# Three instead of four VectorE steps to narrow a weight in the first network, and sums of y on GpSimd

## The chip, the cores and the metric

The kernel runs on one core of one Trainium2 chip, in one launch. The metric is the device time of that launch in microseconds; the median of three runs of the kernel before is 980.27 (979.51 to 982.97).

## The reference

Three stages follow one another; the change is about the weights of the second.

```python
# 1: attention, q k v of (2, 8, 576, 64), with a bias from positions
scores = q @ k.T / 8 + relu(x @ w1 + b1) @ w2
x = softmax(scores) @ v                      # as (1152, 512)
# 2: first network: w_in (512, 2048), w_out (2048, 512), a of 4, b of 2
h = x @ w_in
P = a[0] + a[1]*h + a[2]*h**2 + a[3]*h**3
Q = 1 + abs(b[0])*abs(h) + abs(b[1])*h**2
y = (P / (Q + 1e-6)) @ w_out
# 3: four experts, each w1 (512, 1024) and w2 (1024, 512)
out = sum(p[:, e:e+1] * (relu(y @ w1[e]) @ w2[e]) for e in range(4))
```

w_in and w_out reach the kernel as float64 (their values are float32 times a float64 scale), so on the chip each weight is two 32-bit words. The kernel has to narrow each to a float32 and then to split that into a high and a low part of the matmul type, since every product is three matmuls: high by high, high by low, low by high.

## The kernel before

Every engine's instructions stand in the order in which the Python code records them (manual_schedule), and each engine takes its own in that order. TensorE is called PE, VectorE DVE, ScalarE ACT, GpSimd POOL, and SP issues the DMAs.

**Narrowing** (`Piece.narrow`). A piece of a weight is loaded as `words`, low and high word side by side. Four steps of a piece make the float32 in the tile `narrow`, and a fifth, `split` (L434, L435), writes the two parts: ACT copies the high part, POOL subtracts for the low part. For the 14 weights that are narrowed in the first network (pieces of 128 x 1024):

- step 0: ACT takes Abs of the high words, read as floats (L421);
- step 1: DVE takes the maximum with a small constant (L423, the max step), then shifts left by 3 and clears the upper two bits (L424, the mask step);
- step 2: DVE shifts the low words right by 29 and joins them (L426, the low-word step);
- step 3: DVE joins the upper two bits of the high words (L428, the high-word step).

The first two weights are narrowed early, during attention, in six pieces of one row block each (four of 128 x 256, two of 128 x 512). There step 0 is ACT's Square of the high words into a tile `size` (L418) and DVE's mask step out of `words` (L419), steps 1 and 2 are the low-word and the high-word step, and step 3 sets to zero what was too small (L430, with `size`). `EARLY` gives each step of each piece a unit of the attention; `early_convert` calls it, and with step 2 it asks for the load of the next piece, into the same buffer, which waits until the last reader of the words before is done.

**First network.** 24 units (`units`, index i), each one chunk c of 384 tokens and one block f2 of 256 columns of w_in. A unit is 24 matmuls of `hp` (`first`), then ACT and DVE steps on 128 x 768 elements, then 24 matmuls of `yp` two units later (`second`, LAG = 2). Per unit, in the order of the code: ACT L898 and L899 (qd and u out of hp), ACT L837 and POOL L838 for the unit before (its g, high and low part), DVE L903, L904, L905, ACT L906, L907 and L909 (Abs, Ln, Exp, which give 1/Q), then `convert(STEPS[i][0])`, the matmuls `yp` and `gather`, then DVE L919, L920, L921 (g), then `convert(STEPS[i][1])`. L921 is the last reader of hp, of which there are two buffers, so the matmuls of unit i + 2 wait for it. `convert(n)` takes the next n steps of five of the weight that is due; (3, 2) is one whole weight in a unit: three steps ahead of L919, the split and the next weight's step 0 behind L921. That is so in 12 units (2, 3, 4, 6, 7, 9, 10, 11, 14 to 17); units 0 and 1, and 12 and 13, share one weight each; 5 and 8 have none; from 18 on the float32 weights of the experts are split.

**Sums of y** (`gather`). A chunk's yp in PSUM is added up over a run of units, and then goes to `yacc`. In the first run of a chunk ACT copies it there (L861), in the last DVE adds it out of PSUM (L863) and `result` splits the sum for the experts (L875, L876). In the three runs between (they are gathered in units 8, 12 and 14) ACT copies four times into `new` (L868) and DVE adds two pairs (L871, 128 x 768).

**Third stage.** From about 578 us on PE runs without gaps through the experts.

```python
    STEPS = [(3, 2) if i in (2, 3, 4, 6, 7, 9, 10, 11, 14, 15, 16, 17) else (0, 5 * (i > 17)) for i in range(len(units) + LAG)]
    STEPS[:2] = (2, 0), (1, 2)
    STEPS[12:14] = (2, 0), (1, 2)
```

## Time and profile before

| what | value |
|---|---|
| three runs | 979.51, 980.27, 982.97 us |
| profiled execution: its own time, its span | 981.26 us, 979.3 us |
| PE busy | 880.0 us, 90% |
| DVE busy | 563.9 us, 58% |
| ACT busy | 464.3 us, 47% |
| POOL busy | 191.4 us, 20% |
| mean granted PE clock | 0.958 |

The span goes from the first to the last instruction that the profiler recorded; the execution's own time is 1.96 us longer. Busy shares are averages over stages with different limits. A row of the timeline gives start, length, engine, line, operation, tiles written and read, their shapes and how many instructions run together; the bracket behind it gives the idle time of the engine ahead of the row and what ended it. Where the next instruction of an engine starts before the one ahead has ended, the distance of the starts is what counts.

### The profile page before, as it was taken

Reading aid. Unit: us, or ns where it says so; the run is one execution under the profiler, and the core shown is the slowest. Engines: PE = TensorE matmul, PEld = TensorE weight load, DVE = VectorE, ACT = ScalarE, POOL = GpSimd, SP = SyncE. Lnnn points to the kernel's source line nnn. Section 1 sums busy time; section 2 is a strip of 40 time slices with the busy share of each in tenths; the row PEclk is TensorE's granted clock in tenths of the full one; section 3 lists DMA queues with packets and bytes.
Section 4 is the critical chain, followed back from the end, with each engine's and each line's share of the span. In section 5 each row is a group of like instructions: output and inputs, shape, how many; then the busy total and the mean of one; then the engine's idle time right before and its main releaser. Section 6 shows DMA issues by size and latency. Waiting matters only on the chain.

```text
span 979.3 us, 13056 instructions
## 1 busy us (share of the span) xinstructions
PE 880.0 (90%) x5012; PEld 821.5 (84%) x5012; DVE 563.9 (58%) x876; ACT 464.3 (47%) x771; POOL 191.4 (20%) x217
## 2 busy tenths in 40 slices
PE   6866775799999969988979989999999999999998
PEld 6866774699888869877879989998998899889987
DVE  3666775588999788888989974122222331232111
ACT  3735554589888677866767643122211121121000
POOL 3000013475554433424343210000000000000000
PEclk7978897799999979999999999999999999999999
DMA  4255556423231212213130212012201210020000
GB/s 109 61 142 148 182 202 174 113 56 73 63 87 44 87 43 87 86 53 120 48 126 22 65 44 86 1 44 65 65 1 41 67 65 1 24 63 7 27 33 33
DMA packets 72553, 69.92 MB, mean 71 GB/s; under 512 B 42412, under 2 KB 51116, under 8 KB 72492
## 3 DMA queue, kind: packets, MB, share of 16 engines
q1 hardware_dynamic: 72492, 69.09, 23.7%
q8 instruction: 40, 0.66, 0.3%
q14 instruction: 21, 0.17, 0.1%
HBM read 45.48 MB, written 2.36 MB: 49 GB/s over the span
## 4 chain that ended last, share of the span: by engine, by line
PE 53%; DVE 22%; DMA 10%; ACT 9%; SPq 3%; issue 3%; DVEq 0%; ACTq 0%
PE hp L66 23%; PE op L66 20%; PE bps L66 5%; DMA bc<-ev 3%; DMA xt<-in_c_x_dram 3%; DMA ba<-ev 2%; DVE pq L524 2%; DVE narrow L426 2%; DVE u L905 2%; DVE qd L903 2%; DVE pt L565 2%; DVE narrow L428 2%; DVE u L904 2%; PE sc L66 2%; SPq L298 2%
## 5 line engine op out<-in xcount | busy, mean ns | idle before, releaser
L66 PE MATMUL hp<-x,wi 128*128 128x384 f32 x1656 | 295.6, 336 | 24.0 <-DVE u L921 24.0
L66 PEld LDWEIGHTS hp<-x,wi 128*128 128x128 f32 x1656 | 288.5, 189 | 29.2 <-issue 27.3
L66 PE MATMUL op<-w,h_hi 128*128 128x512 f32 (+1 forms) x592 | 178.4, 384 | 0.0
L884 ACT ACTIVATE h_hi<-hp 128x768 fp32r<-128x768 f32 x48 | 39.1, 814 | 246.5 <-PE hp L66 246.5
L885 DVE SCALAR_TENSOR_TENSOR h_lo<-hp,h_hi 128x768 fp32r<-128x768 f32 x48 | 46.0, 958 | 156.3 <-ACT h_hi L884 156.3
L66 PEld LDWEIGHTS op<-w,h_hi 128*128 128x128 f32 x592 | 110.0, 188 | 21.4
L66 PE MATMUL bps<-mask,wb 128*128 128x288 f32 x472 | 84.8, 344 | 36.2 <-DVE mask L254 21.8
L66 PE MATMUL op<-w,h_lo 128*128 128x512 f32 (+1 forms) x296 | 113.7, 384 | 0.0
L66 PEld LDWEIGHTS bps<-mask,wb 128*128 128x128 f32 x472 | 78.9, 229 | 40.6 <-ACT ev L281 14.4
L66 PE MATMUL yp<-g_hi,w 128*128 128x384 f32 x384 | 101.7, 335 | 1.7 <-ACT y L868 1.6
L956 DVE SCALAR_TENSOR_TENSOR acc<-op,pr_sb,acc 128x512 f32<-128x512 f32 (+1 forms) x28 | 20.5, 732 | 112.8 <-PE op L66 112.8
L66 PE MATMUL sc<-ks,qs 128*128 128x288 f32 x320 | 63.5, 327 | 10.4 <-DVE nm L524 7.2
L66 PEld LDWEIGHTS yp<-g_hi,w 128*128 128x128 f32 x384 | 69.7, 188 | 2.7 <-ACT y L868 2.2
L66 PEld LDWEIGHTS op<-w,h_lo 128*128 128x128 f32 x296 | 55.6, 188 | 11.0
L254 DVE TENSOR_SCALAR mask<-lw,thr 128x576 fp32r<-128x576 f32 x118 | 55.9, 524 | 14.5 <-PE bps L66 13.7
L66 PE MATMUL yp<-g_lo,w 128*128 128x384 f32 x192 | 64.2, 334 | 0.0
L66 PEld LDWEIGHTS sc<-ks,qs 128*128 128x128 f32 x320 | 47.5, 199 | 17.5 <-DVE nm L524 10.5
L838 POOL TENSOR_TENSOR g_lo<-u,g_hi 128x768 fp32r<-128x768 f32 x24 | 44.7, 1861 | 89.3 <-ACT g_hi L837 59.7
L281 ACT ACTIVATE ev<-bps 128x576 f32<-128x576 f32 x59 | 38.4, 650 | 48.6 <-PE bps L66 35.2
L524 DVE CUSTOM_DVE_ANT_0 pq<-sc,ba 128x576 f32<-128x576 f32 x72 | 53.8, 749 | 8.1 <-PE sc L66 6.3
L534 ACT ACTIVATE pq<-pq,nm 128x576 f32<-128x576 f32 x72 | 55.4, 769 | 4.2 <-DVE nm L524 3.8
L565 DVE TENSOR_TENSOR pt<-tp,pt 128x512 fp32r<-128x512 f32 x72 | 49.2, 684 | 9.0 <-ACT pt L564 8.4
(134 smaller groups left out, 1279.6 us busy)
## 6 DMA issues: line engine op xcount, KB each, us to landing
stage<-in_moe_w_dram SPq DMA_DIRECT2D x32, 512.0 KB
ba<-ev SPq DMA_DIRECT2D x32, 288.0 KB
bc<-ev SPq DMA_DIRECT2D x32, 288.0 KB
words<-in_moe_w_in_dram SPq DMA_DIRECT2D x7, 1024.0 KB
words<-in_moe_w_out_dram SPq DMA_DIRECT2D x7, 1024.0 KB
raw_q<-in_q_dram SPq DMA_DIRECT2D x32, 128.0 KB
raw_k<-in_k_dram SPq DMA_DIRECT2D x16, 128.0 KB
raw_v<-in_v_dram SPq DMA_DIRECT2D x16, 128.0 KB
```

The costliest lines, as they stand in the source:

```text
L66: pe.matmul(o, lhsT=l, rhs=r, start=start, stop=stop)
L254: dve.tensor_scalar(mk, win, at, None, ALU.is_gt)
L281: act.activation(e_out, sc[:, :, :288], AF.Copy)
L298: sp.dma_start(dst[:, h], ev[r:r + 29:4])
L426: dve.scalar_tensor_tensor(out=u, in0=lo, scalar=29, in1=u, op0=ALU.logical_shift_right, op1=ALU.bitwise_or)
L524: dve.tensor_tensor_reduce(out=self.row(u).rearrange("p (a j) -> p a j", a=2), in0=sc[:, :, :288], in1=bs.rearrange("p (a j) -> p a j", a= ...
L534: act.activation(self.row(u), self.row(u), AF.Exp, bias=least.pop((self.n, u)), scale=-1.0, accum_out=self.sm[b][:, u - 4 * b:u - 4 * b + 1])
L565: dve.tensor_tensor(lo, tp, f32(hi), ALU.subtract)
L838: pool.tensor_tensor(lo, u, f32(hi), ALU.subtract)
L884: act.activation(hi, h, AF.Relu)
L885: dve.scalar_tensor_tensor(out=lo, in0=h, scalar=0.0, in1=f32(hi), op0=ALU.max, op1=ALU.subtract)
L956: dve.scalar_tensor_tensor(out=acc[:, j, cols], in0=op, scalar=pr_sb[:, j, e:e + 1], in1=acc[:, j, cols], op0=ALU.mult, op1=ALU.add)
```

## The change

Step by step:

- Abs on ACT gets a scale of 2**-111, so that what was too small falls to zero by itself. The max step goes, and the mask step clears one bit instead of two. This form now serves the early pieces too: Square, `size` and the step with L430 go, and their mask step moves from step 0 to step 1, the low-word step from 1 to 2, the high-word step from 2 to 3. A tile `gap` takes the room of `size`.
- Weights come out 2**8 too large. The constants of P and Q absorb that: one DVE instruction on them becomes four, one ACT instruction two. What leaves yp is scaled by 2**-8, in the instructions that copied or added it anyway.
- The adds of L871 go from DVE to POOL.
- `STEPS[0]` goes from (2, 0) to (0, 2): in unit 0 the mask and the low-word step come behind L921 instead of ahead of L919.

```diff
--- before.py
+++ after.py
@@ -22,7 +22,7 @@
 E, FE = 4, 1024
 EXP_AND_LN = [s.name for s in SETS].index("natural_log_exp_and_others")
 
-LEAST, ZERO = (float(np.array(x, np.uint32).view(np.float32)) for x in (0x38100000, 0x38000000))
+SHIFT, WUP = 2.0 ** -111, 2.0 ** 8
 P = 128
 NPAIR = H // 2
 LW_W = 2 * S - 1
@@ -405,29 +405,25 @@
 
         def narrow(self, step):
 
+
+
+
+
+
             if not self.w.w64:
                 return
-            tile_of = lambda name: pools["w"].tile(self.shape, F32, tag=name, name=name, bufs=pools["words"] if name == "narrow" else 1)
             if step == 0:
-                self.raw = tile_of("narrow")
+                self.raw = pools["w"].tile(self.shape, F32, tag="narrow", name="narrow", bufs=pools["words"])
             lo, hi = self.words[:, :, :, 0], self.words[:, :, :, 1]
             st, u = self.raw, self.raw.bitcast(U32)
-
-            if step == 0 and self.early:
-                self.size = tile_of("size")
-                act.activation(self.size, hi.bitcast(F32), AF.Square)
-                dve.tensor_scalar(u, hi, 3, 0x3FFFFFFF, ALU.logical_shift_left, ALU.bitwise_and)
-            elif step == 0:
-                act.activation(st, hi.bitcast(F32), AF.Abs)
-            if step == 1 and not self.early:
-                dve.tensor_scalar(st, st, ZERO, None, ALU.max)
-                dve.tensor_scalar(u, u, 3, 0x3FFFFFFF, ALU.logical_shift_left, ALU.bitwise_and)
-            if step == 2 - self.early:
+            if step == 0:
+                act.activation(st, hi.bitcast(F32), AF.Abs, scale=SHIFT)
+            if step == 1:
+                dve.tensor_scalar(u, u, 3, 0x7FFFFFFF, ALU.logical_shift_left, ALU.bitwise_and)
+            if step == 2:
                 dve.scalar_tensor_tensor(out=u, in0=lo, scalar=29, in1=u, op0=ALU.logical_shift_right, op1=ALU.bitwise_or)
-            if step == 3 - self.early:
-                dve.scalar_tensor_tensor(out=u, in0=hi, scalar=0xC0000000, in1=u, op0=ALU.bitwise_and, op1=ALU.bitwise_or)
-            if step == 3 and self.early:
-                dve.scalar_tensor_tensor(out=st, in0=self.size, scalar=LEAST * LEAST, in1=st, op0=ALU.is_ge, op1=ALU.mult)
+            if step == 3:
+                dve.scalar_tensor_tensor(out=u, in0=hi, scalar=0x80000000, in1=u, op0=ALU.bitwise_and, op1=ALU.bitwise_or)
 
         def split(self):
             t = self.w.t[:, self.rows]
@@ -483,6 +479,7 @@
     qkv0, sp_, pt1, qk1, ap, pools["w"], qkv1, sums = (pool_of(name) for name in ("qkv0", "scores", "pt1", "qk1", "attn", "early", "qkv1", "sums"))
     qkv = (qkv0, qkv0), (qk1, qkv1)
     sums.tile([P, 136], F32, name="gap", bufs=1)
+    pools["w"].tile([P, 512], F32, name="gap", bufs=1)
     pt0 = pool_of("pt0")
     pools["words"] = 1
 
@@ -764,8 +761,11 @@
     sp.dma_start(cb_sb, cb.unsqueeze(0).to_broadcast([P, 2]))
     cst = const.tile([P, 8], F32, name="cst")
     nca, abs_b, one = cst[:, 0:4], cst[:, 4:6], cst[:, 6:7]
-    dve.tensor_scalar(nca, ca_sb, -1.0, None, ALU.mult)
-    act.activation(abs_b, cb_sb, AF.Abs)
+
+    for j in range(4):
+        dve.tensor_scalar(nca[:, j:j + 1], ca_sb[:, j:j + 1], -WUP ** -j, None, ALU.mult)
+    for j in range(2):
+        act.activation(abs_b[:, j:j + 1], cb_sb[:, j:j + 1], AF.Abs, scale=WUP ** -(j + 1))
     dve.memset(one, 1.0 + 1e-6)
 
     def ready(w):
@@ -827,7 +827,7 @@
     g_of, y_of = {}, {}
 
     STEPS = [(3, 2) if i in (2, 3, 4, 6, 7, 9, 10, 11, 14, 15, 16, 17) else (0, 5 * (i > 17)) for i in range(len(units) + LAG)]
-    STEPS[:2] = (2, 0), (1, 2)
+    STEPS[:2] = (0, 2), (1, 2)
     STEPS[12:14] = (2, 0), (1, 2)
 
     def parts(i):
@@ -858,17 +858,17 @@
         for d in range(4):
             ya = yacc[:, d, CHN * c:CHN * c + CHN]
             if i == first_end[c]:
-                act.activation(ya, yp[d][:, :CHN], AF.Copy)
+                act.activation(ya, yp[d][:, :CHN], AF.Copy, scale=1 / WUP)
             elif i == last_end[c]:
-                dve.tensor_tensor(ya, ya, yp[d][:, :CHN], ALU.add)
+                dve.scalar_tensor_tensor(out=ya, in0=yp[d][:, :CHN], scalar=1 / WUP, in1=ya, op0=ALU.mult, op1=ALU.add)
                 later.append(lambda ya=ya, yt=x_t[d][:, c]: result(ya, yt))
             else:
                 if d % 2 == 0:
                     new = tmp("y")
-                act.activation(new[:, d % 2], yp[d][:, :CHN], AF.Copy)
+                act.activation(new[:, d % 2], yp[d][:, :CHN], AF.Copy, scale=1 / WUP)
                 if d % 2:
                     ya = yacc[:, d - 1:d + 1, CHN * c:CHN * c + CHN]
-                    dve.tensor_tensor(ya, ya, new, ALU.add)
+                    pool.tensor_tensor(ya, ya, new, ALU.add)
 
     def result(ya, yt):
 
```

What this moves is shown at three places. First POOL in the first network, from the low part of g of unit 11 to that of unit 14; `wi` is the low part of a weight (L435, now L431), `yacc` and `y` belong to the adds. Before:

```order
L838 TENSOR_TENSOR g_lo<-u,g_hi 128x768 x2
L435 TENSOR_TENSOR wi<-narrow,wi 128x4x256
L838 TENSOR_TENSOR g_lo<-u,g_hi 128x768
L435 TENSOR_TENSOR wi<-narrow,wi 128x4x256
L838 TENSOR_TENSOR g_lo<-u,g_hi 128x768
```

And now:

```order
L838 TENSOR_TENSOR g_lo<-u,g_hi 128x768
L871 TENSOR_TENSOR yacc<-yacc,y 128x2x384 x2
L838 TENSOR_TENSOR g_lo<-u,g_hi 128x768
L431 TENSOR_TENSOR wi<-narrow,wi 128x4x256
L838 TENSOR_TENSOR g_lo<-u,g_hi 128x768
L871 TENSOR_TENSOR yacc<-yacc,y 128x2x384 x2
L431 TENSOR_TENSOR wi<-narrow,wi 128x4x256
L838 TENSOR_TENSOR g_lo<-u,g_hi 128x768
```

The two adds of unit 12 now stand between the g_lo of unit 11 and that of unit 12 (those of unit 8 in the same way ahead of its g_lo); the two of unit 14 stand ahead of the low part of a weight and of g_lo.

Second DVE in units 0 and 1, from the first step of unit 0 on. Before:

```order
L903 SCALAR_TENSOR_TENSOR qd<-qd,cst,hp 128x768
L904 TENSOR_TENSOR u<-hp,u 128x768
L905 SCALAR_TENSOR_TENSOR u<-u,cst,hp 128x768
L423 TENSOR_SCALAR narrow<-narrow 128x1024
L424 TENSOR_SCALAR narrow<-narrow 128x1024
L426 SCALAR_TENSOR_TENSOR narrow<-words,narrow 128x1024
L919 SCALAR_TENSOR_TENSOR qd<-qd,hp 128x768
L920 SCALAR_TENSOR_TENSOR hp<-u,cst,hp 128x2x384
L921 SCALAR_TENSOR_TENSOR u<-qd,hp 128x768
L903 SCALAR_TENSOR_TENSOR qd<-qd,cst,hp 128x768
```

And now (the mask step is now L422, the low-word step L424):

```order
L903 SCALAR_TENSOR_TENSOR qd<-qd,cst,hp 128x768
L904 TENSOR_TENSOR u<-hp,u 128x768
L905 SCALAR_TENSOR_TENSOR u<-u,cst,hp 128x768
L919 SCALAR_TENSOR_TENSOR qd<-qd,hp 128x768
L920 SCALAR_TENSOR_TENSOR hp<-u,cst,hp 128x2x384
L921 SCALAR_TENSOR_TENSOR u<-qd,hp 128x768
L422 TENSOR_SCALAR narrow<-narrow 128x1024
L424 SCALAR_TENSOR_TENSOR narrow<-words,narrow 128x1024
L903 SCALAR_TENSOR_TENSOR qd<-qd,cst,hp 128x768
```

L921 of unit 0 has lost the narrowing ahead of it, and L903 of unit 1 now has two steps of it ahead.

Third ACT in the attention, where the fourth early piece is split and the fifth begins; the brackets name the engines whose semaphores an instruction waits for (DMAHW is a load). Before:

```order
L434 ACTIVATE w<-narrow 128x256 [waits DVE_49]
L534 ACTIVATE pq,sm<-pq,nm 128x576 [waits DVE_49,Activation_49]
L564 ACTIVATE pt<-tp 128x4x128 [waits PE_49]
L195 ACTIVATE qs<-tp_q 128x640 [waits PE_49]
L418 ACTIVATE size<-words 128x512 [waits DMAHW1_49]
L534 ACTIVATE pq,sm<-pq,nm 128x576 [waits DVE_49]
```

And now:

```order
L430 ACTIVATE w<-narrow 128x256 [waits DVE_49]
L531 ACTIVATE pq,sm<-pq,nm 128x576 [waits DVE_49,Activation_49]
L561 ACTIVATE pt<-tp 128x4x128 [waits PE_49]
L195 ACTIVATE qs<-tp_q 128x640 [waits PE_49]
L420 ACTIVATE narrow<-words 128x512 [waits DMAHW1_49,Pool_49]
L531 ACTIVATE pq,sm<-pq,nm 128x576 [waits DVE_49]
```

The step writes `narrow` itself, of which there is one in the attention, so it waits for POOL's subtraction of the piece before; until now DVE's L419 did.

## Rows read from the trace of the kernel before

**Rows 1.** Busy time by engine, 380 to 480 us.

```profile
core 0: us, PE busy (x) PEld busy (x) DVE busy (x) ACT busy (x) POOL busy (x), PEclk, DMA share, GB/s
380.00:480.00 100.00, 85.75 (x481) 82.49 (x480) 88.46 (x95) 72.19 (x89) 36.61 (x18) 1.00 0.23 76
```

**Rows 2.** Timeline of DVE, unit 11 and the first step of unit 12.

```profile
452.84 1.01 DVE L903 SCALAR_TENSOR_TENSOR qd<-qd,cst,hp 128x768 f32<-128x768 f32 x1 [1.03 <-ACT u L899]
...
455.69 0.69 DVE L423 TENSOR_SCALAR narrow<-narrow 128x1024 f32<-128x1024 f32 x1
456.41 0.69 DVE L424 TENSOR_SCALAR narrow<-narrow 128x1024 uint32<-128x1024 uint32 x1
...
458.40 1.23 DVE L428 SCALAR_TENSOR_TENSOR narrow<-words,narrow 128x1024 uint32<-128x1024 uint32 x1
...
463.43 1.02 DVE L903 SCALAR_TENSOR_TENSOR qd<-qd,cst,hp 128x768 f32<-128x768 f32 x1 [1.02 <-ACT u L899]
```

**Rows 3.** Timeline of ACT, end of unit 11.

```profile
459.65 1.06 ACT L434 ACTIVATE wi<-narrow 128x1024 fp32r<-128x1024 f32 x1 [2.98 <-DVE narrow L428]
460.62 1.11 ACT L421 ACTIVATE narrow<-words 128x1024 f32<-128x1024 f32 x1
```

**Rows 4.** Timeline of PE, the matmuls hp that start in unit 10.

```profile
451.95 4.42 PE L66 MATMUL hp<-x,wi 128*128 128x384 f32 x24 [2.09 <-DVE u L921]
```

**Rows 5.** The tile narrow over the whole span: durations as min/median/max in ns.

```profile
L423 DVE TENSOR_SCALAR narrow<-narrow x14: 684/686/689, 348.3 to 516.7; 128x1024 f32<-128x1024 f32 x14
...
L419 DVE TENSOR_SCALAR narrow<-words x6: 281/353/855, 244.7 to 320.8; 128x256 uint32<-128x256 uint32 x4, 128x512 uint32<-128x512 uint32 x2
L430 DVE SCALAR_TENSOR_TENSOR narrow<-size,narrow x6: 414/821/1057, 251.3 to 327.7; 128x256 f32<-128x256 f32 x4, 128x512 f32<-128x512 f32 x2
```

**Rows 6.** Timeline of DVE: adds of units 8, 12, 14, and the unit behind each.

```profile
427.06 1.83 DVE L871 TENSOR_TENSOR yacc<-yacc,y 128x768 f32<-128x768 f32 x2 [1.73 <-ACT y L868]
...
431.59 1.01 DVE L903 SCALAR_TENSOR_TENSOR qd<-qd,cst,hp 128x768 f32<-128x768 f32 x1
...
468.87 1.82 DVE L871 TENSOR_TENSOR yacc<-yacc,y 128x768 f32<-128x768 f32 x2
...
473.40 1.01 DVE L903 SCALAR_TENSOR_TENSOR qd<-qd,cst,hp 128x768 f32<-128x768 f32 x1
...
488.04 1.82 DVE L871 TENSOR_TENSOR yacc<-yacc,y 128x768 f32<-128x768 f32 x2
...
492.57 1.01 DVE L903 SCALAR_TENSOR_TENSOR qd<-qd,cst,hp 128x768 f32<-128x768 f32 x1
```

**Rows 7.** Timeline of ACT: u of unit 9, copies of y in unit 14.

```profile
428.44 1.02 ACT L899 ACTIVATE u<-hp,cst 128x768 f32<-128x768 f32 x1
...
485.12 1.62 ACT L868 ACTIVATE y<-yp 128x384 f32<-128x384 f32 x4
```

**Rows 8.** Timeline of DVE: L876 in unit 19, and once more behind unit 23.

```profile
539.82 3.60 DVE L876 TENSOR_TENSOR x<-yacc,x 128x384 fp32r<-128x384 f32 x4
...
588.40 1.96 DVE L876 TENSOR_TENSOR x<-yacc,x 128x384 fp32r<-128x384 f32 x4
```

**Rows 9.** Timeline of POOL, unit 19.

```profile
540.15 1.92 POOL L838 TENSOR_TENSOR g_lo<-u,g_hi 128x768 fp32r<-128x768 f32 x1 [7.14 <-ACT g_hi L837]
```

**Rows 10.** Timeline of PE, the matmuls hp of unit 2.

```profile
353.95 6.75 PE L66 MATMUL hp<-x,w 128*128 128x384 f32 x24 [7.50 <-DVE u L921]
```

**Rows 11.** Timeline of DVE, start of unit 2.

```profile
362.55 1.01 DVE L903 SCALAR_TENSOR_TENSOR qd<-qd,cst,hp 128x768 f32<-128x768 f32 x1 [1.99 <-ACT u L899]
```

**Rows 12.** Timeline of ACT: Square of the third and the fifth early piece.

```profile
271.24 0.43 ACT L418 ACTIVATE size<-words 128x256 f32<-128x256 f32 x1
...
299.49 0.68 ACT L418 ACTIVATE size<-words 128x512 f32<-128x512 f32 x1
```

**Rows 13.** Timeline of POOL: subtraction of the fourth early piece.

```profile
299.52 0.74 POOL L435 TENSOR_TENSOR w<-narrow,w 128x256 fp32r<-128x256 f32 x1
```

**Rows 14.** Timeline of SP: issue of the third early piece's load.

```profile
266.64 0.35 SPq L401 DMA_DIRECT2D words<-in_moe_w_in_dram  x1
```

**Rows 15.** Busy time by engine, behind the second piece's load (issued at 249.57).

```profile
252.00:253.00 1.00, 0.69 (x6) 0.43 (x4) 1.00 (x4) 0.69 (x3) 0.50 (x2) 1.00 0.01 2
```

## The prediction

> **What bounds the kernel now.** I read the chain that ended last first: through attention it changes hands all the time, from about 345 to 578 us it runs through VectorE and ScalarE, and behind that through PE alone, without a gap. So a microsecond gained in the first network arrives at the end whole, and one gained in the third stage could only come from PE, which the change does not touch. Then I read the busy time in the first network: between 380 and 480 us DVE is busy 88%, PE 86%, ACT 72% and POOL 37% [rows 1]. Two engines are close; which one ends last is told by the waits. PE waits 2.09 us for DVE's last step of a unit before it may write hp again [rows 4], in a unit of 10.59 us (452.84 to 463.43, [rows 2]), so it needs some 8.5 us per unit and is not the bound. DVE waits 1.02 us per unit for ACT's u [rows 2], and ACT before that had waited 2.98 us for DVE's high-word step [rows 3]. That is a loop: first step of a unit on DVE, its three steps, the narrowing steps, the high-word step (458.40), ACT's split (459.65), ACT's Abs for the next weight (460.62), ACT's two reads of hp, first step of the next unit (463.43). A narrowing step on DVE lies on it in full; L919 to L921 lie beside it.
>
> **The change, part by part.**
>
> The max step. From its start to that of the mask step are 455.69 to 456.41, 0.72 us [rows 2], on the loop. It runs 14 times with hardly any spread [rows 5]: 12 in the units that narrow a whole weight, one each in units 0 and 12, which are counted below. 12 x 0.72 = **8.64 us**. What is next is the rest of the same loop, 9.87 us per unit, still over PE's 8.5. The mask step keeps its form, and the scale in Abs is an immediate, so I price it at nothing: Abs lies on the loop, and if a scale made it longer, each hundredth of a microsecond would cost 0.14 in all.
>
> The adds in unit 8, where nothing is narrowed. They hold DVE from 427.06 and unit 9 begins at 431.59 [rows 6]. Without them ACT's u is last: it starts at 428.44 and takes 1.02 [rows 7], so unit 9 begins at 429.5, **2.1 us** earlier. PE gets L921 earlier by as much and is then back to back for a unit, which its spare time in the units around covers.
>
> The adds in unit 12. Unit 13 begins at 473.40 without any wait in its row, so DVE was last there. The two adds (1.82 us, overlapping by about 0.08) and the max step leave: 1.74 + 0.72 = **2.46 us**.
>
> The adds in unit 14. Unit 15 too began when DVE came free (492.57, [rows 6]). Without adds and max step, the loop ends last: the high-word step would start at about 488.04 - 1.2 - 0.72 = 486.1, and from its start to the next unit are 458.40 to 463.43, 5.03 us [rows 2], so 491.2. But POOL now adds just then. The second copy of y ends about 486.0 (four of some 0.4 us from 485.12, [rows 7]), so the first add is waiting when the low-word step ends, ahead of the high-word step. What that does is shown by L876, a DVE instruction with two inputs in SBUF like the high-word step: four of them take 1.96 us alone and 3.60 while POOL subtracts g_lo (540.15 for 1.92), which came when the first of them was running [rows 8, 9]. The extra 1.64 us are nearly all of POOL's instruction: POOL went ahead of the second one, which then waited for it. I take the same here: add of 1.86 us from 486.1, high-word step at 487.95, unit 15 at 487.95 + 5.03 = 492.98, 0.41 later than before instead of the 0.72 earlier counted above, a correction of **+1.13 us**. That DVE gets its turn ahead of the second add I take from symmetry; no row shows it.
>
> The Trainium skill says the same against this move in general: in "GPSIMD Engine Reference", section 8, GpSimd shares its SBUF interfaces with VectorE and contends with VectorE instructions that have two SBUF inputs or run in a two-port mode. It names no order and no price. If by that rule the high-word step stood behind both adds, unit 15 would begin 1.9 later still and the sum below would be 11.3 instead of 13.2; the rows are with it as far as L876 goes.
>
> g_lo behind the adds. In unit 8 the adds (two of 1.86 from 427.1) end at 430.8, and g_lo follows until 432.7; the mask step of unit 9 would start at 429.5 + 2.84 = 432.3 (2.85 is 452.84 to 455.69, [rows 2]). If it waits like L876, **+0.3 us**. In unit 12 the adds end near 472 and g_lo is due then. The yp matmuls, which need g_lo, stand behind a whole hp on PE in both places.
>
> Unit 0. The mask and the low-word step (456.41 to 458.40, 1.99 us, [rows 2]) move behind L921. PE's hp of unit 2 waits 7.50 us for that L921 [rows 10], and unit 2 begins at 362.55 after ACT's u [rows 11]. L921 comes some 1.5 us earlier (2.7 of narrowing less the wait for Exp). Unit 1 starts about 0.35 later, and its high-word step with it; from there the loop takes 5.03 as above, so unit 2 begins at about 356.9 + 5.03 = 361.9: **0.6 us** gained, bounds 0 and 1.5.
>
> Attention. DVE loses L430, six of 0.41 to 1.06 us, median 0.82, and has the mask step (0.28 to 0.86, [rows 5]) one step later, in the place of the low-word step, and so on. At most all six count: 4.9 us; but PE, ACT and DVE share the chain here. Against it stand two waits. ACT's Abs now waits for POOL's subtraction of the piece before: the fifth piece's would start at 299.49, POOL is busy from 299.52 for 0.74 [rows 12, 13], so 0.8 us, in ACT ahead of an Exp for which PE waits. And the next piece's load is released by the high-word step, now one step later, with the loads of q and k behind it in SP's queue; these are due a whole pair of heads later. For the third piece, the one with the fewest units between, it goes out not at 266.64 [rows 14] but at about 268.6, 2.6 us before the Abs at 271.24 [rows 12]; the second's load, issued at 249.57, was through by 252.0 (DMA share 0.01 from there, [rows 15]), 2.4 us. It just fits. I take **0.8 us** gained, one L430, between a loss of 0.8 and a gain of 4.9. The longer instructions on the constants stand where ACT and DVE wait for PE: nothing; without that cover some 0.5.
>
> Sum: 8.64 + 2.1 + 2.46 - 1.13 - 0.3 + 0.6 + 0.8 = 13.2 us. The profiled execution's own time, 981.26, becomes 968.1; it lies 1.0 above the median of the runs, so I predict **967.1**.
>
> **The rivals.**
>
> A. More is gained (0.20): the high-word step slips in ahead of POOL in unit 14 (1.8 more), the mask step of unit 9 does not wait (0.3), and three L430 count instead of one (1.7): 963.3. For it: the margin in unit 14 is only 0.1 us. Against: L876 waited.
>
> B. Another engine becomes the bound (0.17): PE's 8.5 per unit against DVE's and ACT's short units 5, 8 and 12, or POOL, which passes the adds' time on to g_lo and the weights. Then the adds (4.6 us with the max step of unit 12) bring nothing, and about 8.5 remain: 971.8. Against: PE's 2.09 us of waiting per unit and POOL's 37%.
>
> C. The change does not do on the loop what I say (0.06): Abs with a scale, or the copies with a scale, take longer and the max step's 0.72 is eaten in good part. 0.5 us more on each Abs would leave 13.2 - 7 = 6; 0.7 leave 3.4: 977.
>
> D. Slower (0.02): in attention, ACT's new wait for POOL. It decides if POOL's queue is late: five pieces have one before them, and each wait would have to reach 3.6 us to turn 13.2 into a loss of 5, about 985. The subtraction of the fourth piece is only 0.77 late for it [rows 12, 13].
>
> **How the numbers follow.** My forecast has 0.55, A 0.20, B 0.17, C 0.06, D 0.02. A measurement of this kernel tells about 0.5%, 4.9 us, from no change. Forecast, A and B are faster by more: 0.92; C within: 0.06; D slower: 0.02. The ends of the unknown costs put together are 13.2 + 2.1 + 4.1 + 0.9 = 20.3 and 13.2 - 1.9 - 1.6 - 0.6 = 9.1 us; all at one end at once is unlikely above, so the range goes from 962 to 972, which takes in A and B.
>
> **What would show it.** The distance from one first step of a unit to the next is about 9.9 in units 2, 3, 10 and 15, with DVE still waiting 1.0 us for ACT's u, and PE's wait for L921 at about 1.4; units 8 and 12 take 7.1 and 7.5 us. In unit 14 the high-word step lasts about 3 us instead of 1.2, and the unit some 11.6; a high-word step of 1.2 there is rival A. Unit 2 begins 0.6 earlier against unit 0. In attention ACT waits for POOL at the fifth piece, and the first network starts 0.8 earlier. I am wrong if the units stay at 10.6, or if PE stops waiting for L921.

## The result, and the profile after

The changed kernel takes 964.89 us (median of four runs, 961.70 to 966.89) beside 979.89 for the kernel before: ratio 0.9861, 95% interval 0.9825 to 0.9897, so 15.0 us less; forecast were 13.2 less and 967.1. In the profiled execution (its own time 963.71, span 961.8) TensorE is still the busiest engine; DVE is busy 13.8 us less and POOL, which has the adds now, 11.0 us more. The page's busy times and its row for the matmuls of hp:

```profile
PE 878.7 (91%) x5012; PEld 821.6 (85%) x5012; DVE 550.1 (57%) x853; ACT 463.6 (48%) x772; POOL 202.4 (21%) x223
...
L66 PE MATMUL hp<-x,wi 128*128 128x384 f32 x1656 | 294.3, 335 | 13.8 <-DVE u L921 13.7
```

The second row is the one that tells: PE's idle time ahead of hp (its last two numbers), nearly all of it put down to DVE's L921, was 24.0 us and is 13.8. The same row of the kernel before:

```profile
L66 PE MATMUL hp<-x,wi 128*128 128x384 f32 x1656 | 295.6, 336 | 24.0 <-DVE u L921 24.0
```

By engine and stretch, a hundred microseconds of the first network, units 2 to 13 (those of [rows 1] were 3 to 13):

```profile
362.00:462.00 100.00, 92.82 (x522) 89.71 (x521) 87.89 (x92) 79.26 (x103) 46.78 (x23) 1.00 0.26 85
```

DVE stays at 88% although each unit asks less of it, since the units are shorter; POOL went from 37 to 47%. One whole-weight unit on DVE, unit 10, which answers to [rows 2]:

```profile
431.50 1.01 DVE L903 SCALAR_TENSOR_TENSOR qd<-qd,cst,hp 128x768 f32<-128x768 f32 x1 [1.11 <-ACT u L899]
...
434.35 0.69 DVE L422 TENSOR_SCALAR narrow<-narrow 128x1024 uint32<-128x1024 uint32 x1
435.07 1.22 DVE L424 SCALAR_TENSOR_TENSOR narrow<-words,narrow 128x1024 uint32<-128x1024 uint32 x1
436.33 1.23 DVE L426 SCALAR_TENSOR_TENSOR narrow<-words,narrow 128x1024 uint32<-128x1024 uint32 x1
...
441.38 1.01 DVE L903 SCALAR_TENSOR_TENSOR qd<-qd,cst,hp 128x768 f32<-128x768 f32 x1 [1.05 <-ACT u L899]
```

From first step to first step 9.88 us, with the same wait of 1.05 for ACT's u at its end: the loop is the same, one step shorter. PE's wait, 2.09 in [rows 4], is now 1.32 ahead of the hp that starts in unit 11, a unit of 9.87 (in unit 10, two behind the short unit 8, it is 0.72):

```profile
450.37 1.82 PE L66 MATMUL hp<-x,wi 128*128 128x384 f32 x9 [1.32 <-DVE u L921]
```

Unit 14 is the place where DVE and POOL meet. Timeline of DVE and then of POOL there:

```profile
466.71 1.02 DVE L903 SCALAR_TENSOR_TENSOR qd<-qd,cst,hp 128x768 f32<-128x768 f32 x1 [1.11 <-ACT u L899]
...
470.28 1.23 DVE L424 SCALAR_TENSOR_TENSOR narrow<-words,narrow 128x1024 uint32<-128x1024 uint32 x1
471.54 2.81 DVE L426 SCALAR_TENSOR_TENSOR narrow<-words,narrow 128x1024 uint32<-128x1024 uint32 x1
...
478.23 1.01 DVE L903 SCALAR_TENSOR_TENSOR qd<-qd,cst,hp 128x768 f32<-128x768 f32 x1 [1.10 <-ACT u L899]
```

```profile
471.42 4.64 POOL L871 TENSOR_TENSOR yacc<-yacc,y 128x768 f32<-128x768 f32 x2 [2.07 <-ACT y L868]
476.03 2.38 POOL L431 TENSOR_TENSOR wi<-narrow,wi 128x1024 fp32r<-128x1024 f32 x1
```

The high-word step takes 2.81 us instead of 1.23, and the two adds take 4.64 where the same two take 3.65 in unit 8 (there DVE does nothing else with two SBUF inputs):

```profile
419.06 3.65 POOL L871 TENSOR_TENSOR yacc<-yacc,y 128x768 f32<-128x768 f32 x2 [2.08 <-ACT y L868]
```

So each waited for the other once. In attention ACT shows the two waits that the prediction looked at, ahead of the Abs of the third and of the fifth early piece ([rows 12] has the Square in their place, without a wait); the third piece's load was issued at 265.84:

```profile
269.08 0.44 ACT L420 ACTIVATE narrow<-words 128x256 f32<-128x256 f32 x1 [0.92 <-POOL raw_k L187]
...
297.35 0.68 ACT L420 ACTIVATE narrow<-words 128x512 f32<-128x512 f32 x1 [0.69 <-POOL w L431]
```

The time by place, in us, from one profiled execution of each kernel. Units are from L903 to the next L903; "network" is from unit 0 to unit 23; "attention" from unit 33 of the attention's 72 (ahead of the first early step that the change touches) to unit 0; "third" from unit 23 to the end of the span; the last column is when attention unit 12 starts.

| kernel | units 0+1 | 8 | 10 | 12 | 14 | 15 | network | attention | third | start of att. 12 |
|---|---|---|---|---|---|---|---|---|---|---|
| before | 17.06 | 9.19 | 10.60 | 9.97 | 11.23 | 10.66 | 225.58 | 104.58 | 408.17 | 193.3 |
| changed | 16.43 | 7.16 | 9.88 | 7.50 | 11.52 | 9.92 | 212.78 | 103.62 | 407.26 | 190.6 |
| max step back | 18.66 | 7.16 | 10.61 | 8.23 | 12.20 | 10.66 | 224.71 | 103.72 | 408.76 | 192.9 |
| adds on DVE | 16.42 | 9.19 | 9.87 | 9.24 | 10.49 | 9.93 | 215.43 | 103.77 | 409.58 | 194.0 |
| first add on DVE | 16.43 | 7.16 | 9.88 | 7.49 | 11.29 | 9.93 | 212.50 | 103.62 | 408.71 | 190.0 |
| late adds | 16.42 | 7.16 | 9.88 | 7.50 | 9.94 | 11.77 | 212.99 | 103.53 | 408.74 | 199.1 |
| STEPS[0] back | 15.74 | 7.15 | 9.88 | 7.49 | 11.53 | 9.93 | 212.12 | 103.57 | 408.84 | 188.9 |
| four half adds | 16.41 | 7.15 | 9.88 | 7.49 | 10.63 | 10.10 | 211.96 | 103.65 | 406.84 | 190.2 |
| extra early step | 16.42 | 7.16 | 9.89 | 7.50 | 11.50 | 9.93 | 212.75 | 106.05 | 407.25 | 188.5 |
| one add a unit | 16.41 | 7.15 | 9.87 | 7.50 | 9.94 | 9.94 | 211.16 | 103.50 | 413.00 | 187.8 |
| early units | 16.41 | 7.16 | 9.88 | 7.50 | 11.51 | 9.93 | 212.74 | 102.05 | 407.27 | 187.4 |
| wide copy target | 16.42 | 7.16 | 9.88 | 7.50 | 9.95 | 9.94 | 211.32 | 103.70 | 413.82 | 185.4 |
| combined | 15.40 | 7.15 | 9.88 | 7.49 | 9.95 | 9.94 | 210.26 | 102.00 | 406.84 | 197.1 |
| changed, again | 16.42 | 7.16 | 9.88 | 7.50 | 11.54 | 9.93 | 212.80 | 103.56 | 408.63 | 189.3 |

Two things are to be read from it. Units repeat to some 0.05 us, network and attention to 0.3, so what an edit does there is seen in one profile. But attention unit 12 starts anywhere from 185 to 199 us in kernels whose instructions ahead of it are the same: there the chain of waits runs through DMA transfers of up to 15 us, and in each run through others, of other lengths. Three pieces of it in the kernel before, and one in the changed kernel (start, length, what):

```profile
92.35 15.18 DMA xt<-in_c_x_dram
...
121.32 11.21 DMA xt<-in_c_x_dram
...
146.09 11.45 DMA bc<-ev
```

```profile
111.46 11.77 DMA ba<-ev
```

That is most of the scatter of the totals. Of the 17.5 us between the two profiled spans, 12.8 are the network, 1.0 is attention, 0.9 the third stage, and 2.8 lie ahead of attention unit 12.

### The profile page after: what moved, and what is told of

Read it like the earlier page. It is cut to its first block, busy times and chain, and to the rows that moved or that the text cites. A ratio compares the mean times of both kernels' runs of the same rounds, so it can differ in the third digit from the quotient of the medians.

```text
span 961.8 us, 13043 instructions
## 1 busy us (share of the span) xinstructions
PE 878.7 (91%) x5012; PEld 821.6 (85%) x5012; DVE 550.1 (57%) x853; ACT 463.6 (48%) x772; POOL 202.4 (21%) x223
## 4 chain that ended last, share of the span: by engine, by line
PE 53%; DVE 18%; DMA 11%; ACT 10%; issue 4%; SPq 3%; POOL 0%; DVEq 0%; ACTq 0%; POOLq 0%
PE hp L66 22%; PE op L66 20%; DMA ba<-ev 8%; PE bps L66 3%; DVE qd L903 2%; DVE narrow L426 2%; PE sc L66 2%; DVE u L904 2%; DVE narrow L424 2%; SPq L298 2%; DVE pq L521 2%; PE o L66 2%; ACT u L899 2%; DVE pt L562 2%; ACT narrow L420 2%
## 5 line engine op out<-in xcount | busy, mean ns | idle before, releaser
L66 PE MATMUL hp<-x,wi 128*128 128x384 f32 x1656 | 294.3, 335 | 13.8 <-DVE u L921 13.7
L254 DVE TENSOR_SCALAR mask<-lw,thr 128x576 fp32r<-128x576 f32 x118 | 56.7, 531 | 13.1 <-PE bps L66 12.3
```

Of the source, the lines that this page charges most:

```text
L66: pe.matmul(o, lhsT=l, rhs=r, start=start, stop=stop)
L254: dve.tensor_scalar(mk, win, at, None, ALU.is_gt)
```

## The experiments

All are edits of the changed kernel. The theory: a loop of DVE and ACT through the narrowing steps sets the unit; adds on POOL are free except where they meet a DVE instruction with two SBUF inputs. The rivals: another engine has become the bound, unit 14 is long for another reason, or the gain comes from places that the change does not touch.

### The max step back

```diff
             if step == 1:
+                if not self.early:
+                    dve.tensor_scalar(st, st, 0.0, None, ALU.max)
                 dve.tensor_scalar(u, u, 3, 0x7FFFFFFF, ALU.logical_shift_left, ALU.bitwise_and)
```

> The changed kernel with one more VectorE step ahead of the mask step, a maximum with 0 that changes no value. Theory (a loop of VectorE and ScalarE through the narrowing steps sets the unit): every whole-weight unit grows from about 9.9 to 10.6 us, 11 of them by 0.72; unit 12 by 0.72 too; unit 14 by nothing, since there the high-word step waits for GpSimd's first add anyway and comes 0.7 later into that wait; units 0 and 1 together by 0 to 0.7. Sum +8.6 to +9.4, so about 974. Rival (TensorE or GpSimd has become the bound since): less than 5 us, and the 1.0 us that VectorE waits for ScalarE's u shrinks.

976.45 us (973.26 to 979.66), ratio to before 0.9980 (0.9951 to 1.0008). The eleven other whole-weight units grow by 0.73 on average, unit 12 by 0.73, and DVE keeps waiting 1.1 for ACT's u: the rival falls. But the network grows by 11.93, not by 8.6 to 9.4. Unit 14 took 0.68 more where I expected nothing: the low-word step comes 0.72 later and still has 0.8 us to run when POOL's first add is due. The add waits for it and is then as much in the way of the high-word step (2.75 us) as before. The two adds take 5.30 us together:

```profile
482.70 5.30 POOL L873 TENSOR_TENSOR yacc<-yacc,y 128x768 f32<-128x768 f32 x2 [2.08 <-ACT y L870]
```

Unit 18 took 0.27 more, whose cause stays open, and unit 0 alone took 2.24 more. In unit 0 the low-word step, 0.72 later than in the changed kernel, now comes just behind POOL's g_lo instead of just ahead of it. DVE, then POOL there (from the added step on, lines are 2 further on than in the changed kernel):

```profile
352.38 2.73 DVE L426 SCALAR_TENSOR_TENSOR narrow<-words,narrow 128x1024 uint32<-128x1024 uint32 x1
```

```profile
351.97 2.06 POOL L840 TENSOR_TENSOR g_lo<-u,g_hi 128x768 fp32r<-128x768 f32 x1 [8.16 <-ACT g_hi L839]
```

In the changed kernel the low-word step started at 349.14, before g_lo at 349.45, and took 1.23; there g_lo took 2.61. Who starts first goes first.

### The adds on DVE again

```diff
-                    pool.tensor_tensor(ya, ya, new, ALU.add)
+                    dve.tensor_tensor(ya, ya, new, ALU.add)
```

> The changed kernel with the adds of L871 on VectorE again. Theory (adds beside the loop are free on GpSimd except in unit 14, where they hold up the high-word step): unit 8 +2.0, unit 12 +1.75, unit 14 from 11.5 to about 10.5, with a high-word step of 1.2 again; sum +2.8, about 967.7. Rival (unit 14 is long for another reason, the change of the narrowing): unit 14 stays at 11.5 or grows; sum +3.8 or more. Rival (GpSimd passes the time on): no change.

968.61 us (965.27 to 972.39), ratio 0.9896 (0.9859 to 0.9932). Unit 8 +2.03, unit 12 +1.74, unit 14 down to 10.49 with a high-word step of 1.23; the network +2.65. As the theory said, to 0.15 us. So the move to POOL is worth 2.03 + 1.74 and costs 1.03 in unit 14. The same step as in unit 14 of the changed kernel, without POOL's adds:

```profile
478.81 1.23 DVE L426 SCALAR_TENSOR_TENSOR narrow<-words,narrow 128x1024 uint32<-128x1024 uint32 x1
479.95 1.82 DVE L871 TENSOR_TENSOR yacc<-yacc,y 128x768 f32<-128x768 f32 x2
```

### Shared bandwidth, or turns: the first add on DVE

```diff
-                    pool.tensor_tensor(ya, ya, new, ALU.add)
+                    (dve if i == 12 and d == 1 else pool).tensor_tensor(ya, ya, new, ALU.add)
```

(i is the unit whose yp is gathered, two behind: 12 is gathered in unit 14.)

> The changed kernel with the first of the two adds of unit 14 on VectorE, the second stays on GpSimd. If the two engines only share bandwidth: high-word step 1.2, add on VectorE about 1, unit 14 9.9 to 10.1, 1.5 us less than 964.9. If one engine's whole instruction holds the other off: the high-word step takes 1.2, but GpSimd's add is due when it ends, so VectorE's own add lasts about 2.8 instead of 0.95, L919 starts near the same time as now, and unit 14 takes 11.5 to 11.8: nothing gained.

964.25 us (963.92 to 965.95), ratio 0.9865 (0.9829 to 0.9901). Half the work taken from POOL gains 0.23 us in unit 14 (11.29, a little under the 11.5 to 11.8 that I expected of turns, and far from the 9.9 to 10.1 of shared bandwidth): the high-word step is short again, and DVE's own add, of 0.95, takes its place as the one that waits. DVE, then POOL:

```profile
470.95 1.23 DVE L426 SCALAR_TENSOR_TENSOR narrow<-words,narrow 128x1024 uint32<-128x1024 uint32 x1
472.09 2.62 DVE L871 TENSOR_TENSOR yacc<-yacc,y 128x768 f32<-128x768 f32 x1
```

```profile
471.59 2.31 POOL L871 TENSOR_TENSOR yacc<-yacc,y 128x768 f32<-128x768 f32 x1 [2.82 <-ACT y L868]
473.85 3.10 POOL L431 TENSOR_TENSOR wi<-narrow,wi 128x1024 fp32r<-128x1024 f32 x1
```

Four instructions in turn: high-word on DVE, add on POOL, add on DVE, L431 on POOL, each of POOL's two longer than alone (1.86 and 2.38), and DVE's add by 1.67.

### The same adds as four halves

```diff
-                    ya = yacc[:, d - 1:d + 1, CHN * c:CHN * c + CHN]
-                    pool.tensor_tensor(ya, ya, new, ALU.add)
+                    for k in range(2):
+                        yk = yacc[:, d - 1 + k, CHN * c:CHN * c + CHN]
+                        pool.tensor_tensor(yk, yk, new[:, k], ALU.add)
```

> The changed kernel with each pair of adds on GpSimd written as two instructions of half the size (128x384, about 0.95 us each). If the high-word step of unit 14 waits for the one GpSimd instruction that runs when it is due, and then has its turn: it takes 1.22 + 0.95 or a little less, about 2.1 instead of 2.81, and unit 14 about 10.8 instead of 11.5. If GpSimd keeps the port until its queue of adds is done: over 4 us, unit 14 over 13. If the two share the port at a lower rate: about 2.8 and 11.5, as now.

One run, 962.18 us. The high-word step takes 1.92, unit 14 10.63. One half add was waited for, and not all four; expected were about 2.1 and 10.8:

```profile
471.13 1.92 DVE L426 SCALAR_TENSOR_TENSOR narrow<-words,narrow 128x1024 uint32<-128x1024 uint32 x1
```

This settles the step that the prediction took "from symmetry": DVE gets its turn between two POOL instructions. Four halves hold POOL 0.63 longer in all (5.27 against 4.64 us in unit 14), and the g_lo behind them meets the mask step of unit 15, which takes 0.86 instead of 0.69 us; that is the 0.18 by which unit 15 is longer. DVE, then POOL there:

```profile
479.78 0.86 DVE L422 TENSOR_SCALAR narrow<-narrow 128x1024 uint32<-128x1024 uint32 x1
```

```profile
478.20 1.89 POOL L838 TENSOR_TENSOR g_lo<-u,g_hi 128x768 fp32r<-128x768 f32 x1
```

The network is 0.8 shorter than with two adds.

### The adds behind the low part of the weight

```diff
+                    add = lambda ya=ya, new=new: pool.tensor_tensor(ya, ya, new, ALU.add)
+                    if i == 12:
+                        late.append(add)
+                    else:
+                        add()
...
             convert(STEPS[i][1])
+            while late:
+                late.pop(0)()
```

> The changed kernel with the two adds of unit 14 on GpSimd recorded behind the low part of the weight, which itself waits for the high-word step. Theory (the adds cost only because they meet the high-word step): high-word step 1.2, unit 14 9.9 instead of 11.5, the adds run beside L919 to L921, which read hp in PSUM and are not held up; unit 15 unchanged within 0.3; 1.3 to 1.6 us less, about 963.4. Rival (any two-input VectorE instruction is held up, or g_lo of unit 14 comes too late for TensorE): the 1.6 us come back in L919 to L921 or in unit 15.

969.43 us (963.88 to 973.78), ratio 0.9897 (0.9860 to 0.9933), network 212.99. Here the rival was right about the place, though not about the reason: unit 14 is 9.94, and unit 15 takes 1.85 more instead. POOL's adds and g_lo ran into the next weight. POOL, then DVE in unit 15:

```profile
484.77 3.66 POOL L871 TENSOR_TENSOR yacc<-yacc,y 128x768 f32<-128x768 f32 x2
488.38 2.27 POOL L838 TENSOR_TENSOR g_lo<-u,g_hi 128x768 fp32r<-128x768 f32 x1
```

```profile
487.95 1.03 DVE L422 TENSOR_SCALAR narrow<-narrow 128x1024 uint32<-128x1024 uint32 x1
489.02 2.71 DVE L424 SCALAR_TENSOR_TENSOR narrow<-words,narrow 128x1024 uint32<-128x1024 uint32 x1
```

Both narrowing steps waited for POOL: the mask step, 1.03 instead of 0.69 us, for the end of the adds, and the low-word step, 2.71 instead of 1.23, for the rest of g_lo. The three steps of unit 15 from its first on, which have hp in PSUM as an input, ran beside the adds at their usual 1.01, 0.95 and 1.01 us.

### One add a unit

Between the end of the high-word step and the next mask step are some 6.5 us. One add, L431 and g_lo take 1.86 + 2.4 + 1.86 = 6.1. A copy of one element that reads what the high-word step wrote keeps the add from starting ahead of it.

```diff
+    gate = mp.tile([P, 1], F32, tag="gate", name="gate", bufs=1)
...
             gather(i - LAG)
+        if late:
+            raw = under_way[state["done"]].raw
+            pool.tensor_copy(gate, raw[:, 0, :1])
+            late.pop(0)()
```

(Adds of i == 12 go into `late` as before, and nothing is popped behind convert.)

> The changed kernel with the two adds of unit 14 put one each into units 14 and 15, each behind a copy of one element per partition on GpSimd that reads what the high-word step wrote, so that no add can start ahead of it. Then GpSimd's add (1.86), the weight's low part (2.4) and g_lo (1.86) fit between the end of the high-word step and the next mask step, 6.5 us: high-word steps 1.2, units 14 and 15 both 9.9, 1.6 us less than now. Rival (the small copy costs far more than its size, or g_lo runs into the next mask and low-word step as in the kernel with the late adds): unit 15 or 16 at 10.3 or more, and part of the 1.6 comes back.

One run, 965.66 us. Units 14 and 15 are 9.94 each, the network 211.16, 1.62 less than changed. The theory held for the network; but the third stage took 413.00 us, instead of 406.8 to 409.6 in twelve other profiles. The page's row for its matmuls shows a mean of 389 ns, in the changed kernel 384 (the granted clock is 1.00 in both between 660 and 760 us):

```profile
L66 PE MATMUL op<-w,h_hi 128*128 128x512 f32 (+1 forms) x592 | 181.8, 389 | 0.0
```

```profile
L66 PE MATMUL op<-w,h_hi 128*128 128x512 f32 (+1 forms) x592 | 178.4, 384 | 0.0
```

The tile `gate` has moved all tiles behind it in its pool (wi, words, narrow, and the buffers of g and h) by 32 bytes. So once more with 128 bytes:

```diff
-    gate = mp.tile([P, 1], F32, tag="gate", name="gate", bufs=1)
+    gate = mp.tile([P, 32], F32, tag="gate", name="gate", bufs=1)
```

> The kernel with one add per unit once more, with the tile for the one-element copy 128 bytes wide per partition instead of 4. In the run with 4 bytes the third stage took 413.0 us instead of 407 to 409.6, every matmul of op being 5 to 10 ns longer. If the 4 bytes did it by moving the tiles behind them to other addresses: the third stage takes 407 to 409 again, units 14 and 15 stay at 9.9, the first network at 211.2. Rival (that run was on a slower chip or in a disturbed state, or GpSimd's copy does it): the rival cannot be excluded by a third stage of 407 to 409, but one of 413 would exclude the address.

One run, 963.88 us, third stage 413.82. My expectation had it that 413 would exclude the address. That was wrong: this tile moves the others too, by 128 bytes. A slower chip is not the cause: on the chip of the first of the two runs other kernels took 406.8 to 409.6, and on that of the second 407.27 (early units). The combined run below separates the rest.

### STEPS[0] as it was

```diff
-    STEPS[:2] = (0, 2), (1, 2)
+    STEPS[:2] = (2, 0), (1, 2)
```

> The changed kernel with STEPS[0] = (2, 0) again, so that in unit 0 the mask and the low-word step stand ahead of L919. The prediction gave the move 0.6 us: units 0 and 1 together would take 17.06 again instead of 16.43. Rival (the max step alone did it): L921 of unit 0 comes 0.72 earlier than in the kernel before, TensorE's hp of unit 2 and ScalarE's u follow it, and units 0 and 1 take 17.06 - 0.72 = 16.3, as little as with the move; the move then brings nothing. All other units as in the changed kernel.

One run, 962.92 us. Units 0 and 1 take 15.74, less than the 16.43 with the move and less than the rival's 16.3: in this run the move costs 0.69. The first step of unit 1 starts 7.49 us behind that of unit 0 instead of 8.53: ahead of L919 the two steps, 1.87 us from start to start, delay it by only 0.83 (it starts 4.71 behind the first step instead of 3.88), since it waits for ACT's Exp anyway, while behind L921 they stand in full ahead of unit 1. What the move does shorten is PE's wait, 5.93 us instead of 6.77. Windows over the hp behind that wait, STEPS[0] back and then changed (the third number from the end is the mean granted clock; 1.00 is 2.4 GHz, 0.50 is 1.2 GHz):

```profile
347.77:353.94 6.17, 6.17 (x25) 6.17 (x26) 6.10 (x7) 5.43 (x6) 3.01 (x2) 0.69 0.18 36
```

```profile
348.65:354.39 5.74, 5.74 (x25) 5.74 (x26) 5.67 (x7) 3.35 (x5) 2.61 (x1) 0.75 0.00 0
```

The hp is longer here, at a lower clock, but not because of the longer wait. In the eleven profiles that have the move, with 5.92 to 5.94 us of wait, the same hp takes anything from 5.74 to 7.17 us, at a clock of 0.75 to 0.58, and behind 6.76 us of wait in the combined kernel it takes 5.83, at 0.73. One add a unit, then combined:

```profile
345.81 7.17 PE L66 MATMUL hp<-x,w 128*128 128x384 f32 x24 [5.93 <-DVE u L930]
```

```profile
354.41 5.83 PE L66 MATMUL hp<-x,w 128*128 128x384 f32 x24 [6.76 <-DVE u L929]
```

What decides the clock there stays open. With the move the length does not matter: units 0 and 1 take 16.41 to 16.43 in all ten profiles that have it and not the max step, because the loop through unit 1 ends last. Without the move the end of hp comes last, and the time of the two units follows it: 15.74 with 6.17, 15.40 with 5.83. In the kernel before the same hp took 6.75 behind a wait of 7.50 ([rows 10]), at a granted clock of 0.62. So without the move the hp of unit 2 starts 0.73 earlier against unit 0 than before, by the max step, and takes 0.58 less, which no edit is shown to have done: 1.31 of the 1.32 us between 17.06 and 15.74. With the mean length of the eleven, 6.47 us, units 0 and 1 would take about 16.05 without the move; the move then costs 0.4 us, an estimate.

### L430's time back in attention

```diff
+                if self.early:
+                    dve.scalar_tensor_tensor(out=st, in0=st, scalar=1.0, in1=st, op0=ALU.mult, op1=ALU.max)
```

(Behind the high-word step.)

> The changed kernel with one more VectorE step of the old L430's shape behind the high-word step of each of the six early pieces (a maximum of a value with itself). Theory (removing L430 gave the 1.0 us between attention unit 33 and the first network, all else there being equal or a small loss): that stretch grows from 103.6 to about 104.6. Rival (most of L430 was hidden, and the 1.0 came from elsewhere): it stays within 0.3 of 103.6. Upper bound, all six on the chain: 108.5. The first network is unchanged at 212.8.

One run, 964.05 us. The stretch grows by 2.43 to 106.05, not by 1.0. So six steps of 0.43 to 0.83 us (3.6 in all) arrive by two thirds. If taking L430 out brought as much as putting this step in costs, it brought far more than the 0.96 that the stretch shows, and the rest went into new waits. This run also tells what ACT waits for ahead of the third piece's Abs. In the changed kernel the row names POOL's L187; here that instruction runs from 267.03 for 0.87 us, across the start of the Abs, and the wait is for the load, issued at 264.26:

```profile
267.51 0.44 ACT L420 ACTIVATE narrow<-words 128x256 f32<-128x256 f32 x1 [0.47 <-DMA words<-in_moe_w_in_dram]
```

From issue to Abs that is 3.25 us, and 3.24 in the changed kernel.

### Two early steps one unit earlier

```diff
-    EARLY = [divmod(i, 9) for i in (31, 32, 33, 34, 35, 37, 38, 40, 41, 42, 43, 44, 45, 46, 47, 49, 50, 51, 52, 54, 55, 58, 59, 60, 61, 63, 64, 65, 66, 68)]
+    EARLY = [divmod(i, 9) for i in (31, 32, 33, 34, 35, 37, 38, 39, 40, 41, 43, 44, 45, 46, 47, 49, 50, 51, 52, 53, 55, 58, 59, 60, 61, 63, 64, 65, 66, 68)]
```

> The changed kernel with two steps of EARLY in earlier attention units: of the second early piece low-word, high-word and split in units 39, 40, 41 instead of 40, 41, 42, so the third piece's load is released one unit sooner; of the fourth piece the split in unit 53 instead of 54. Theory (removing L430 gives 2.1 to 2.4 us in attention, and two new waits on ScalarE, for the third piece's load and for GpSimd's subtraction ahead of the fifth piece, take 0.7 and 0.4 of it back): the idle times of 0.92 and 0.69 ahead of these two Abs go, and the stretch from attention unit 33 to the first network shrinks from 103.6 to about 102.5. Rival (the waits only stood in for others, or units 39 and 53 have no room): 103.4 to 104. The first network is unchanged at 212.8.

One run, 958.95 us. Attention shrinks to 102.05, by 1.57 and so a little more than expected, and both waits are gone; the third piece's load is now issued at 260.44, 4.3 us ahead of its Abs instead of 3.2:

```profile
264.74 0.44 ACT L420 ACTIVATE narrow<-words 128x256 f32<-128x256 f32 x1
...
292.33 0.69 ACT L420 ACTIVATE narrow<-words 128x512 f32<-128x512 f32 x1
```

Against the kernel before that is 2.53 us, the size of the extra early step's 2.43. The two edits (load, subtraction) were not tried apart, nor were the earlier units tried in the kernel before, where these waits do not exist.

### The findings together

STEPS[0] back, one add a unit, and the early units; the copy's target is a free column of the tile with the constants.

```diff
+            pool.tensor_copy(cst[:, 7:8], raw[:, 0, :1])
...
-    STEPS[:2] = (0, 2), (1, 2)
+    STEPS[:2] = (2, 0), (1, 2)
```

> Three findings put together on the changed kernel: STEPS[0] = (2, 0) again (units 0 and 1 together 15.7 instead of 16.4), one add each in units 14 and 15 behind GpSimd's copy of one element (9.9 each instead of 11.5 and 9.9), and the earlier attention units of two early steps (attention unit 33 to first network 102.05 instead of 103.6). The copied element goes into a free column of the tile with the constants, so that no tile gets another address. Sum -0.7 - 1.55 - 1.55 = -3.8 us, first network 210.5, about 961 against 965 of the changed kernel in this call, ratio to the kernel before 0.982. If the other address of the tiles behind the copy's target made the third stage slow in the two runs before, it takes 407 to 409 here; if GpSimd's copy did it, 413 again, and the gain is gone. Rival for the combination: with (2, 0) the low-word and the high-word step of unit 0 and 1 move against GpSimd, and 0.7 comes back; or moving L431 of the second piece against other GpSimd work in unit 41 costs more.

> The changed kernel once more, unedited, on the same chip as the combined one, for a time of it beside that one and to see how far the first 180 us differ between its own runs. Theory (the first-network intervals are reproduced to 0.1 us, what differs between runs lies ahead of attention unit 12, and in the third stage): first network 212.8, attention unit 33 to it 103.6, ratio 0.984 to 0.988. Rival (the 2.8 us gained ahead of attention unit 12 in its first profile were of the change): attention unit 12 again starts 2 to 3 us earlier than in the kernel before.

Combined: 963.99 us (958.23 to 967.37), ratio to before 0.9845 (0.9806 to 0.9884). Changed, again, on the same chip: 966.13 (963.82 to 969.60), ratio 0.9881 (0.9843 to 0.9919). By place the combined kernel does what was expected: units 14 and 15 at 9.95 and 9.94, units 0 and 1 at 15.40 (15.7 expected; their hp took 5.83 instead of 6.17), network 210.26, attention 102.00, together 4.1 us less than the changed kernel; and the third stage takes 406.84 with matmuls of 384 ns. The copies and adds stand where they stood in the two runs with 413, and the pool's tiles have their old addresses again (the buffers that g and h share are the same thirteen, taken in another order). That leaves the tiles' place as what made the third stage slow in those two runs. Which tile, and why, stays open. POOL in units 14 and 15, where everything now fits:

```profile
476.78 0.19 POOL L923 COPY cst<-narrow 128x1 f32<-128x1 f32 x1 [3.48 <-DVE narrow L426]
476.92 1.86 POOL L871 TENSOR_TENSOR yacc<-yacc,y 128x768 f32<-128x768 f32 x1
478.74 2.40 POOL L431 TENSOR_TENSOR wi<-narrow,wi 128x1024 fp32r<-128x1024 f32 x1
481.38 1.86 POOL L838 TENSOR_TENSOR g_lo<-u,g_hi 128x768 fp32r<-128x768 f32 x1 [0.24 <-POOL wi L431]
```

The medians differ by 2.1 us and their intervals overlap, so the totals alone do not show that it is faster than the changed kernel; the scatter ahead of attention unit 12 (197.1 against 189.3 in these two profiles) is larger than the gain.

The second run of the changed kernel repeats network (212.80) and attention (103.56) within 0.06; its ratio is at the edge of the 0.984 to 0.988 expected. Its attention unit 12 starts at 189.3, 4.0 us ahead of the kernel before; the fourteen profiles run from 185.4 to 199.1, and there is but one of the kernel before. So the 2.8 us ahead of it in the first profile cannot be put down to the change. They are not shown to have nothing to do with it either.

## Why the prediction was right, step by step

**The loop.** Right. It forecast 9.9 us in whole-weight units with DVE still waiting 1.0 for ACT's u, and PE's wait at about 1.4; measured are 9.88, 1.05 and 1.32. The interval of these twelve units falls by 0.73 on average, but for units 9 (0.66) and 14. Rival C (Abs or the copies become longer) did not happen, and neither did B: with the max step back the units follow it by 0.71 to 0.74, the mark of a loop that this step lies on.

**Adds in units 8 and 12.** Right: 2.04 and 2.47 us against 2.1 and 2.46.

**Unit 14.** Right in its mechanism, forecast 11.6, measured 11.52; the high-word step 2.81 against "about 3". That the add would come first was as close as the prediction said: it starts at 471.42, 0.12 us ahead of the high-word step. The symmetry that no row showed is shown by the four half adds and by the first add on DVE: the engines take turns by whole instructions. The Trainium skill states this, on a page that the prediction did not draw on: "SBUF — State Buffer", section "SBUF: two separate sides", calls the ports that VectorE and GpSimd share an exclusive lock, held for the whole instruction by whichever starts first, and no division of bandwidth. The runs agree (2.81, 1.92 and 2.62 us for steps of 1.23, 1.23 and 0.95 alone), and add that between two instructions of POOL that stand back to back a waiting DVE instruction gets in.

**Unit 9.** "+0.3 us" was mis-sized: 0.06. That the mask step would wait as L876 does was right, although it has one input in SBUF and L876 two; what was too large is the overlap. g_lo ended 0.18 us after the start of the mask step, not 0.4, and the mask step took 0.72 instead of 0.69. With 0.31 us of g_lo left it took 0.86 (four half adds), with 0.48 us of the adds left 1.03 (late adds). The steps with two inputs follow the same rule: the low-word step took 1.50 us longer with 1.65 of g_lo left (max step back), DVE's add 1.67 longer with 1.81 of POOL's add left (first add on DVE). In each case the extra time is what is left of POOL's instruction less some 0.15 us.

**Unit 0.** The 0.63 measured where 0.6 was forecast is in part luck. The forecast for the changed kernel was right in its mechanism: with the max step gone and the two steps moved, the loop through unit 1 ends last, unit 2 was to begin 16.4 us behind unit 0, and it does (16.43). But the 0.6 counts from the 17.06 of the kernel before, and those hang on the 6.75 us of one hp [rows 10], which the prediction took as fixed. It is not: behind one and the same wait it took 5.74 to 7.17 us. With an hp of 6.1 us the kernel before would have taken 16.4 too (8.45 to the start of hp, and 1.86 from its end to unit 2; an estimate), and nothing would have been gained. Nor is the gain the move's: the run with the move undone is 0.69 faster still. What one edit of several is worth has to be worked out against the kernel that has the others in it.

**Attention.** "0.8 us, one L430" against 0.96 measured is right in the sum by luck and wrong in its parts. Taking out L430 brought about 2.5, as far as two indirect runs tell (2.43 by the extra step, 2.53 with both waits gone), and two waits took 1.6 of it back. One of the two the prediction had priced at 0.8 ahead of the fifth piece; 0.69 of idle time stands there. The other, the third piece's load, "just fits" by 0.2 us in the prediction, from the second piece's 2.4 us. It did not fit: 3.2 us passed from issue to Abs, 0.92 of them with ACT idle.

**The sum.** Network 12.8 and attention 1.0, together 13.8 where 13.2 was forecast. The 15.0 between the medians has an interval of 10.1 to 17.1 us (by the ratio's), so the remaining 1.2 are within what the runs scatter. In the later call, with the kernel before at a median of 978.40, the difference was 12.3 us.

## What to carry to other kernels

Where DVE and POOL work side by side, list DVE's instructions that have all their tensors in SBUF (here the mask step with one input too) and all of POOL's, as if they were on one engine: a POOL add of 1.86 us is free between two such DVE steps and costs nearly its length in front of one. If the POOL work does not fit into one gap, cut it over two units, and let it begin behind a dependency on the DVE step that it would else hold up. And where whole times scatter by more than an edit is worth, compare the distances between repeated steps of one stage: here they repeat to 0.05 us where the totals of one kernel spread over 5 to 10. And ask how steady a row is before it is taken as a fixed cost: the one hp after the long wait in unit 0 spread over 1.4 us.

## What was not expected of the hardware

- DVE instructions with one input in PSUM pass POOL unhindered: in the fourteen profiles the six steps of a unit that read hp start some 870 times while a subtraction or an add of POOL runs, and all take 0.94 to 1.02 us, as they do alone. The mask step, with its one input in SBUF, does wait (0.86 and 1.03 instead of 0.69).
- Behind the same wait of 5.9 us the same 24 matmuls took 5.74 to 7.17 us in eleven profiles, at a mean granted clock of 0.75 to 0.58.
- With 32 bytes more ahead of a pool's tiles the third stage took some 1% longer (413.0 against 406.8 to 409.6 us; its matmuls 389 against 384 ns, at a granted clock of 1.00 in both), with 128 bytes likewise (413.8); with the old addresses 406.8 came back.
- Transfers in the first 180 us shift the start of attention unit 12 between 185.4 and 199.1 us from run to run, a spread of 13.7 us and so about as much as the whole change is worth.
